# Routing attention and a squared-ReLU feed-forward: the attention stage's instruction order written out by hand for every engine

## The chip, the cores and the metric

The kernel runs on one core of a Trainium2 chip. The metric is device time in microseconds (us); times before are the median of three runs. Five engines work side by side, each through a queue of its own and in the order of that queue: TensorE (PE, with its weight loads as PEld), VectorE (DVE), ScalarE (ACT), GpSimd (POOL) and SyncE (SP), which here issues nearly all DMAs. An instruction that waits for another engine or a transfer holds up what stands behind it in its queue.

## The reference, cut to what matters

Queries and keys of each head are put into 16 clusters by their nearest centroid; a query attends to the keys of its own cluster. The result, with the heads side by side, goes through two matrices with a squared ReLU between.

```python
# q, k, v: (4, 8, 768, 64); centroids: (8, 16, 64); w_in: (512, 2048); w_out: (2048, 512)
q_assign = np.argmax(np.einsum('bhsd,hcd->bhsc', q_n, c_n), axis=-1)     # rows normalized
k_assign = np.argmax(np.einsum('bhsd,hcd->bhsc', k_n, c_n), axis=-1)
mask = q_assign[:, :, :, None] == k_assign[:, :, None, :]
scores = np.where(mask, scale * np.matmul(q, k.transpose(0, 1, 3, 2)), -1e9)
attn = softmax(scores)                       # over the keys
x = np.matmul(attn, v)                       # -> (3072, 512), heads side by side
r = np.maximum(x @ w_in, 0.0)
return (r * r) @ w_out
```

## The kernel before

Attention works on pairs of heads: `NG` = 16 pairs, numbered p, and three steps for each, so step t = 3p + ph with ph = 0, 1, 2. Steps 0 and 1 take 512 queries against half of the keys each, step 2 the other 256 queries against all. A step is: scores (`score_products`, tile sc, three PSUM tiles i = 0 to 2) and the mask added by a second product of one-hot codes (`mask_products`, from ohT), exponentials of the three tiles on ACT (tile ex), and one step later the products with v (`times_v`, tile av), whose result is copied to xT.

Around this, each pair needs:

- its transposed q and k (tile qkT). Pairs 0 and 1 are transposed on PE (`turn_first`, `turn`); the others are split into 16-bit words by ACT (`split_words`, tile flat), written out (words) and read back by a transposing DMA (`turn_words`).
- cluster numbers: `logits` (PE, tile lg, copied by ACT to lgs), then `number`: three transpositions on PE (lt), then on DVE a maximum (mx), two comparisons (best), a maximum (first) and a cast (ids_b). Pairs 0 and 1 turn the one-hot itself on PE (`turn_onehot`, oh to po to ohT). From pair 2 on `spread` transposes the numbers on PE (pb), ACT copies them (row), SP writes them out (far) and reads them back to all partitions (wide), and DVE compares them with each partition's own number (two operations, ohT).
- sums of the exponentials: step 0 on DVE (total), steps 1 and 2 begun on POOL (part) and merged by DVE. `add_up` adds them over the keys on PE (sm), takes the reciprocal on DVE (r), spreads it by DMA (far_r, rb) and scales xT.
- 16 blocks of `w_in` are loaded (w_raw) and rounded meanwhile, each with two ACT passes, three DVE passes and one POOL addition.

PSUM tiles pt, lg, lt, pb, sm and most po share one buffer (`misc`), so each waits until the one before is read.

Behind attention the feed-forward part runs batch by batch in the order 1, 2, 3, 0: `up` with seven half-size products in place of eight (`combine`), sums of blocks of x (x_t, DVE) and of `w_in` (w_s, POOL) as operands, and `down` in the same manner. During the first `up` the 16 blocks of `w_out` are rounded.

What sets the order: under `tc.manual_schedule(engines={PE})` PE's instructions run as written; the dictionary `between` lists what is put between scores and v products of each step (place 0) or behind the v products (place 1). The other engines' order is chosen by a scheduler from the program's order and priorities (`tc.high_priority(offset=200)` raises some), and `tc.issue_after` holds an instruction back behind another.

Of the kernel before, what the change touches and what calls it, by code (L numbers as in the profile page):

```python
# [12 lines left out]
U32 = mybir.dt.uint32  # L13
# [12 lines left out]
def kernel(  # L26
# [57 lines left out]
    BY_PE = 2  # L84
# [52 lines left out]
    def round_block(dst, w):  # L137
        dst = dst.bitcast(U32)
        lo, hi = w[:, :, 0], w[:, :, 1]
        nc.scalar.activation(out=dst.bitcast(F32), in_=hi.bitcast(F32), func=ACT.Abs)  # L140
        nc.scalar.activation(
            out=lo.bitcast(F32), in_=lo, func=ACT.Copy, bias=2.0, scale=2.0 ** -51
        )
        nc.vector.scalar_tensor_tensor(  # L144
            out=lo, in0=hi, scalar=0x80000000, in1=lo, op0=ALU.bitwise_and, op1=ALU.bitwise_or
        )
# [4 lines left out]
        nc.vector.tensor_scalar(  # L151
            out=dst, in0=hi, scalar1=3, scalar2=None, op0=ALU.logical_shift_left
        )
        dst, lo = dst.bitcast(I32), lo.bitcast(I32)
        nc.gpsimd.tensor_tensor(out=dst, in0=dst, in1=lo, op=ALU.add)

    def round_weights(i):
        round_block(weights[i][0] if i < N_IN else w_out[:, i - N_IN], raw_w.pop(i))
# [40 lines left out]
    constants = nc.vector.tensor_scalar(  # L199
        out=cl, in0=row_i[:, 1:2], scalar1=-1.0, scalar2=float(C), op0=ALU.mult, op1=ALU.add  # L200
    ).ins
# [9 lines left out]
    def centroids_norm():  # L211
        sq = once.tile([P, D], F32, name="cen_sq")
        ss = const.tile([P, 1], F32, name="cen_ss")
        with tc.issue_after(constants):
            nc.vector.tensor_tensor(out=sq, in0=cen, in1=cen, op=ALU.mult)
# [47 lines left out]
    def turn(pair, part, spare=False):  # L263
# [6 lines left out]
        nc.scalar.copy(out=qkT[pair][:, 4 * part : 4 * part + 4], in_=pt)  # L270
# [4 lines left out]
    last_exp = [None]  # L275

    def split_words(pair, which):
# [6 lines left out]
        for e in range(2):  # L284
            with tc.issue_after(last_exp[0]) if last_exp[0] else ExitStack():
                nc.scalar.copy(out=flat[:, :, :, D * e : D * (e + 1)], in_=src[:, e])  # L286
# [18 lines left out]
    def logits(pair):  # L305
        if pair >= NG:
            return
# [8 lines left out]
        with tc.high_priority(offset=200):  # L316
            nc.scalar.copy(out=lgs[pair], in_=lg)
# [3 lines left out]
    def number(pair):  # L321
        if pair >= NG:
            return
        lt = misc("lt", [P, NB, P])
        src = lgs.pop(pair)
        for i in range(NB):
            nc.tensor.transpose(out=lt[:, i], in_=src[:, i * P : (i + 1) * P], identity=ident)
# [4 lines left out]
        lt = lt.rearrange("p i (g c) -> p (i g) c", c=C)  # L332
# [4 lines left out]
        with tc.high_priority(offset=200):  # L337
            nc.vector.reduce_max(out=mx, in_=lt, axis=AX.X)
            nc.vector.tensor_tensor(out=best, in0=lt, in1=over_c(mx), op=ALU.is_ge)
            nc.vector.tensor_tensor(  # L340
                out=best, in0=best, in1=order.unsqueeze(1).to_broadcast([P, n, C]), op=ALU.mult
            )
            nc.vector.reduce_max(out=first, in_=best, axis=AX.X)
            if pair < BY_PE:
                nc.vector.tensor_tensor(
                    out=oh.rearrange("p i g e c -> p (i g e) c")[:, :, 0:C], in0=best,
                    in1=over_c(first), op=ALU.is_equal,
                )
            else:
                numbers[pair] = small.tile([P, 2, 4, NB], BF16, name="ids_b")  # L350
                nc.vector.tensor_copy(
                    out=numbers[pair].rearrange("p e g i -> p i g e"),
                    in_=first.rearrange("p (i g e) -> p i g e", i=NB, g=4),
                )

    def turn_onehot(pair, which, spare=False):
        if which == 0:
            ohT[pair] = ohtp.tile([P, 2, S], BF16, name="ohT")
        pt = misc("po", [P, NCH, P], BF16, spare=spare)
        for c in range(NCH):  # L360
            nc.tensor.transpose(
                out=pt[:, c],
                in_=oh[:, c % NB, 2 * which + c // NB].rearrange("p e c -> p (e c)"),
                identity=ident_b,
            )
        dst = ohT[pair][:, which]
        src = pt.rearrange("p c n -> p (c n)")
        if which == 0:
            nc.vector.tensor_copy(out=dst, in_=src)
        else:  # L370
            nc.scalar.activation(out=dst, in_=src, func=ACT.Copy, bias=-BIG, scale=BIG)

    def spread(pair):
        if pair >= NG:
            return
# [7 lines left out]
        wide = once.tile([P, 2, S], BF16, name="wide")  # L383
        ohT[pair] = ohtp.tile([P, 2, S], BF16, name="ohT")
        with tc.high_priority(offset=200):
            nc.scalar.copy(out=row, in_=pb)
            nc.sync.dma_start(far.rearrange("e r n -> (e r) n"), row)
            for e in range(2):
                nc.sync.dma_start(
                    wide[D * e : D * (e + 1)].rearrange("p g n -> p (g n)"),  # L390
                    far[e].rearrange("r n -> (r n)").partition_broadcast(D),
                )
        nc.vector.tensor_scalar(
            out=ohT[pair][:, 0], in0=wide[:, 0], scalar1=cl, scalar2=None, op0=ALU.is_equal
        )
        nc.vector.tensor_scalar(
            out=ohT[pair][:, 1], in0=wide[:, 1], scalar1=cl, scalar2=-BIG,
# [42 lines left out]
    def exponentials(t):  # L440
        ex[t] = []
        for i in range(3):
            ex[t].append(expp.tile([P, 2, 512], F32, name="ex"))
            last_exp[0] = nc.scalar.activation(  # L444
                out=ex[t][i], in_=sc[t][i], func=ACT.Exp, scale=SCALE
            ).ins
        sc.pop(t)
        pair, ph = divmod(t, 3)

        def add(eng, out, a, b):  # L450
            eng.tensor_tensor(out=out, in0=a, in1=b, op=ALU.add)  # L451

        e0, e1, e2 = ex[t]
        if ph == 0:
            total[pair] = endp.tile([P, 2, S], F32, name="total")
            dst = total[pair][:, :, 0:QA]
            add(nc.vector, dst, e0, e1)
            add(nc.vector, dst, dst, e2)
            return
        part = accp.tile([P, 2, 512], F32, name="part")  # L460
        add(nc.gpsimd, part, e0, e1)
        if ph == 1:
            dst = total[pair][:, :, 0:QA]
            add(nc.gpsimd, part, part, e2)
            add(nc.vector, dst, dst, part)
        else:
            add(nc.vector, part, part, e2)
            add(nc.vector, total[pair][:, :, QA:S], part[:, :, 0:QB], part[:, :, QB : 2 * QB])
# [4 lines left out]
    def scores(t):  # L473
        begin(t)
        for todo in pieces(t)[1]:
            score_products(t, todo)
            mask_products(t, todo)
        exponentials(t)
        if t % 3 == 2:
            for d in (qkT, ohT):  # L480
                d.pop(t // 3)
# [29 lines left out]

    def add_up(pair, sm):
# [14 lines left out]
        for e in range(2):  # L527
            nc.sync.dma_start(rb[D * e : D * (e + 1)], far[e].partition_broadcast(D))
        nc.sync.dma_start(seen[4 * pair : 4 * pair + 4], r)
        b, hp = divmod(pair, HP)  # L530
        x = x_of(b)[:, hp]
        nc.vector.scalar_tensor_tensor(
            out=x, in0=x, scalar=UP, in1=rb, op0=ALU.mult, op1=ALU.mult
# [5 lines left out]
    between = {}  # L539

    def put(t, place, work):
        between.setdefault((t, place), []).append(work)

    for i, place in ((0, 0), (1, 0), (2, 0)):
        put(0, 0, lambda i=i: turn(1, i, spare=i == 1))
    put(1, 0, lambda: logits(1))
    put(1, 1, lambda: number(1))
    put(2, 0, lambda: turn_onehot(1, 0))
    put(2, 1, lambda: turn_onehot(1, 1))
    put(3, 0, lambda: logits(2))  # L550
    put(3, 1, lambda: number(2))
    put(4, 0, lambda: spread(2))
    for p in range(NG - 1):
        t = 3 * p
        if p > 1:
            put(t, 1, lambda p=p: spread(p + 1))
        if p > 0:
            put(t + 1, int(p == 1), lambda p=p: add_up(p - 1, misc("sm", [P, TB])))
            put(t + 2, 0, lambda p=p: logits(p + 2))
            put(t + 2, 1, lambda p=p: number(p + 2))  # L560
    put(NT - 2, 0, lambda: add_up(NG - 2, misc("sm", [P, TB])))

    def transfers(t):
        pair, ph = divmod(t, 3)
        if ph == 0:
            load_qk(pair + 3)
            turn_words(pair + 2)
        else:
            split_words(pair + 3, ph - 1)
        if ph == 1:  # L570
            load_v(pair + 1)
        if ph == 2 and pair == HP:
            nc.sync.dma_start(x_far, xT.pop(0))
# [4 lines left out]
    logits(0)  # L578
    number(0)
    begin(0)  # L580
    score_products(0, pieces(0)[1][0])
    turn_onehot(0, 0, spare=True)
    turn_onehot(0, 1)
# [387 lines left out]
```

## Time and profile before

| | |
|---|---|
| median of 3 runs | 1008.78 us (1007.40 to 1010.06) |
| the profiled execution | 1009.22 us, of which the span of its instructions 1007.1 |
| PE busy | 942.0 us, 94% of the span |
| DVE, ACT, POOL busy | 554.8, 304.9, 271.7 us |
| mean granted TensorE clock | 0.977 |
| moved by DMA | 80.06 MB |

Start-up reaches to about 23 us (the scores of step 1), attention to 404.4, the first `up` to about 499, and the rest of the feed-forward part to the end. In rows of the profile L12 is line 12 of the kernel; "out<-in" names tiles; "xN" counts instructions. A view of stretches gives each engine's busy time, then the granted TensorE clock, the mean busy share of the 16 DMA engines and GB/s. In a time line a row has start, duration, engine, line and operation, and in brackets how long the engine stood idle before it and what ended that. In the list of waits a row has engine and line, whom it waited for, the total in us, how often, and the longest.

### The profile page before, as it was taken

The numbers are of one execution on the slowest core, as the hardware profiler recorded it, in microseconds if no ns is written. First come the engines' busy times: TensorE is split into PE (matmuls) and PEld (weight loads), VectorE is DVE, ScalarE is ACT, GpSimd is POOL, SyncE is SP. The second block draws the span as 40 slices with busy tenths as digits, with TensorE's granted clock in tenths as the row PEclk, the third lists the DMA queues.
The fourth block names the chain that finished last, engine by engine and source line by source line (L and its number), as shares of the span: only waits on it lengthen the run. The fifth ranks groups of instructions, "written<-read, shape, count | busy, mean of one in ns | idle before, by whom it ended". The sixth has DMA issues, their size and how long they took to land.

```text
span 1007.1 us, 11663 instructions
## 1 busy us (share of the span) xinstructions
PE 942.0 (94%) x4545; PEld 589.0 (58%) x4545; DVE 554.8 (55%) x809; ACT 304.9 (30%) x461; POOL 271.7 (27%) x217
## 2 busy tenths in 40 slices
PE   6889897988798999988899999999999999999997
PEld 4334343433343444544588755788655888556886
DVE  4356665656476575999822365622455532566321
ACT  4447564555556545443100011000111000111000
POOL 0224343434543344567000333001232002231000
PEclk9999998999999999999899999999999999999999
DMA  8537576757565720341100000000000000000000
GB/s 251 127 111 194 164 238 167 190 159 189 162 175 158 179 65 33 119 121 49 62 22 21 21 0 1 1 21 21 21 1 1 1 21 32 11 0 1 21 21 25
DMA packets 97912, 80.06 MB, mean 79 GB/s; under 512 B 53561, under 2 KB 86713, under 8 KB 97593
## 3 DMA queue, kind: packets, MB, share of 16 engines
q1 hardware_dynamic: 96136, 78.81, 26.9%
q8 instruction: 38, 0.62, 0.3%
q10 hardware_dynamic: 1712, 0.43, 0.2%
q14 instruction: 26, 0.20, 0.1%
HBM read 49.05 MB, written 19.06 MB: 68 GB/s over the span
## 4 chain that ended last, share of the span: by engine, by line
PE 66%; DVE 12%; issue 6%; DMA 6%; POOL 5%; ACT 4%; SPq 1%; ACTq 0%; DVEq 0%; POOLq 0%
PE bank L719 28%; PE bank L685 22%; PE sc L424 8%; PE av L502 5%; POOL part L451 3%; DMA rb<-far_r 2%; ACT ex L444 2%; DMA w_raw<-in_moe_w_out_dram 1%; PE sc L435 1%; DVE g L646 1%; DVE part L451 1%; ACT flat L286 1%; DVE w_raw L144 1%; DMA far<-row 1%; DMA far_r<-r 1%
## 5 line engine op out<-in xcount | busy, mean ns | idle before, releaser
L444 ACT ACTIVATE ex<-sc 128x1024 f32<-128x1024 f32 x144 | 139.2, 1027 | 117.7 <-PE sc L435 117.7
L646 DVE TENSOR_TENSOR g<-bank,g 128x384 f32<-128x384 f32 x192 | 103.4, 553 | 90.2 <-PE bank L685 89.1
L424 PE MATMUL sc<-qkT 64*128 64x512 f32 (+1 forms) x768 | 151.5, 529 | 1.0 <-ACT ex L444 1.0
L502 PE MATMUL av<-ex,v_raw 128*64 128x512 f32 (+1 forms) x768 | 137.1, 499 | 0.7 <-ACT xT L508 0.7
L719 PE MATMUL bank<-w_out,g 128*128 128x256 f32 x576 | 129.5, 384 | 4.4 <-DVE g L630 4.4
L674 POOL TENSOR_TENSOR w_s<-w_in 128x256 f32<-128x256 f32 x32 | 26.9, 842 | 364.6 <-PE bank L719 246.0
L719 PEld LDWEIGHTS bank<-w_out,g 128*128 128x128 f32 x576 | 111.0, 193 | 21.2 <-DVE g L630 4.8
L451 POOL TENSOR_TENSOR part<-ex 128x1024 f32<-128x1024 f32 x32 | 77.4, 2418 | 135.1 <-ACT ex L444 118.5
L646 DVE TENSOR_TENSOR osb<-bank,osb 128x256 f32<-128x256 f32 x72 | 29.4, 423 | 147.8 <-PE bank L719 137.2
L424 PEld LDWEIGHTS sc<-qkT 64*128 64x128 f32 x768 | 72.3, 196 | 57.5 <-issue 46.6
L502 PEld LDWEIGHTS av<-ex,v_raw 128*64 128x64 f32 x768 | 51.5, 138 | 76.5 <-issue 58.9
L685 PE MATMUL bank<-x_t,w_s 128*128 128x384 f32 x256 | 93.3, 487 | 3.1 <-DVE g L646 2.3
L685 PE MATMUL bank<-xT,w_in 128*128 128x384 f32 x256 | 93.5, 488 | 1.4 <-DVE g L646 1.4
L685 PE MATMUL bank<-xT,w_s 128*128 128x384 f32 x256 | 93.3, 487 | 1.1 <-POOL w_s L630 1.1
L719 PE MATMUL bank<-w_t,g 128*128 128x256 f32 x384 | 86.8, 379 | 0.0
L719 PE MATMUL bank<-w_t,g_s 128*128 128x256 f32 x384 | 86.8, 379 | 0.0
L719 PEld LDWEIGHTS bank<-w_t,g_s 128*128 128x128 f32 x384 | 73.0, 190 | 9.9
L719 PEld LDWEIGHTS bank<-w_t,g 128*128 128x128 f32 x384 | 73.0, 190 | 9.9
L650 ACT COPY osb<-bank 128x256 f32<-128x256 f32 x12 | 4.5, 372 | 219.6 <-PE bank L719 219.6
L685 PEld LDWEIGHTS bank<-x_t,w_s 128*128 128x128 f32 x256 | 48.4, 190 | 38.0 <-DVE g L646 3.5
L685 PEld LDWEIGHTS bank<-xT,w_s 128*128 128x128 f32 x256 | 48.4, 190 | 35.9 <-POOL w_s L630 1.7
L685 PEld LDWEIGHTS bank<-xT,w_in 128*128 128x128 f32 x256 | 48.2, 190 | 35.7 <-DVE g L646 2.7
(121 smaller groups left out, 1005.8 us busy)
## 6 DMA issues: line engine op xcount, KB each, us to landing
words<-flat SPq DMA_DIRECT2D x28, 384.0 KB
w_raw<-in_moe_w_in_dram SPq DMA_DIRECT2D x16, 512.0 KB
w_raw<-in_moe_w_out_dram SPq DMA_DIRECT2D x16, 512.0 KB
v_raw<-in_v_dram SPq DMA_DIRECT2D x16, 384.0 KB
rb<-far_r SPq DMA_DIRECT2D x32, 192.0 KB
out_dram<-osb SPq DMA_DIRECT2D x23, 256.0 KB
q_raw<-in_q_dram SPq DMA_DIRECT2D x14, 384.0 KB
k_raw<-in_k_dram SPq DMA_DIRECT2D x14, 384.0 KB
```

The costliest lines, as they stand in the source:

```text
L144: nc.vector.scalar_tensor_tensor(out=lo, in0=hi, scalar=0x80000000, in1=lo, op0=ALU.bitwise_and, op1=ALU.bitwise_or)
L286: nc.scalar.copy(out=flat[:, :, :, D * e : D * (e + 1)], in_=src[:, e])
L424: nc.tensor.matmul(sc[t][i][:, e, cols], lhsT=qkT[pair][rows, NCH + c], rhs=qkT[pair][rows, queries.start // P : queries.stop // P], start ...
L435: nc.tensor.matmul(sc[t][i][:, e, cols], lhsT=ohT[pair][rows, 1, c * P : (c + 1) * P], rhs=ohT[pair][rows, 0, queries], start=False, stop= ...
L444: last_exp[0] = nc.scalar.activation(out=ex[t][i], in_=sc[t][i], func=ACT.Exp, scale=SCALE).ins
L451: eng.tensor_tensor(out=out, in0=a, in1=b, op=ALU.add)
L502: nc.tensor.matmul(av[pair][D * e : D * (e + 1), 0:n], lhsT=raw_v[pair][:, e, c], rhs=e_t[i][:, e, cols], start=c == 0, stop=c == NCH - 1,)
L646: nc.vector.tensor_tensor(out=out, in0=bank, in1=to, op=ALU.add)
L650: nc.scalar.copy(out=c11, in_=bank)
L674: nc.gpsimd.tensor_tensor(out=s1, in0=a[1][0], in1=a[1][1], op=ALU.add)
L685: nc.tensor.matmul(bank, lhsT=operands[j][0][:, kk], rhs=operands[j][1][:, kk], start=(kk == 0), stop=(kk == H2 - 1),)
L719: nc.tensor.matmul(bank, lhsT=operands[j][0][:, f], rhs=operands[j][1][:, f], start=(f == 0), stop=(f == F2 - 1),)
```

## The change

The manual schedule now covers PE, DVE, ACT, POOL and SP, so in attention all five run in the order in which the loop over the steps issues. To make that order, functions are cut up:

- `number` is only the DVE part; its transpositions are `turn_logits`. `number(p + 1)` is issued at the beginning of step 0 of pair p, ahead of that step's scores, right behind `turn_logits` at the end of the step before; `spread(p + 1)` follows between the step's second and third exponential. The comparisons are a function `one_hot`, issued in step 2.
- The merges of POOL's sums are issued one step behind the sums (`merge_second` in step 2, `merge_third` in step 0 of the next pair, behind `number`). Scaling xT (`finish`) is issued in a later pair's step 0 than `add_up`.
- Rounding a block of `w_in` takes three steps, one engine in each (`round_1` ACT, `round_2` DVE, `round_3` POOL), one block for a pair, with the last three blocks in steps 40 to 47.
- `split_words` stands ahead of the exponentials of its step.
- Pair 2 too turns its one-hot on PE (`ONE_HOT` = 3), and `turn_onehot` does both halves between scores and masks. Of the first copies to qkT in `turn`, two of three go to DVE. v of pair 0 is loaded behind q and k of pair 2.
- The sums of x and the first two groups' sums of `w_in` for the first `up` are issued in the last two pairs.
- In the first `up` all four squared ReLUs of a group run on ACT; two of them were on DVE.

On DVE, where a pair's comparisons, sums and numbering meet (before, pairs around the stretch of 105 to 120 us):

```order
L522 RECIPROCAL r<-sm 128x384
L393 TENSOR_SCALAR ohT<-wide,cl 128x768
L396 TENSOR_SCALAR ohT<-wide,cl 128x768
L451 TENSOR_TENSOR total<-total,part 128x2x512
L144 SCALAR_TENSOR_TENSOR w_raw<-w_raw 128x512
L147 TENSOR_SCALAR w_raw<-w_in 128x512
L151 TENSOR_SCALAR w_in<-w_raw 128x512
L532 SCALAR_TENSOR_TENSOR xT<-xT,rb 128x768
L451 TENSOR_TENSOR part<-part,ex 128x1024
L338 TENSOR_REDUCE mx<-lt 128x24
L451 TENSOR_TENSOR total<-part 128x2x256
L339 TENSOR_TENSOR best<-lt,mx 128x384
```

The same place now:

```order
L543 RECIPROCAL r<-sm 128x384
L404 TENSOR_SCALAR ohT<-wide,cl 128x768
L407 TENSOR_SCALAR ohT<-wide,cl 128x768
L456 TENSOR_TENSOR total<-total,part 128x2x512
L347 TENSOR_REDUCE mx<-lt 128x24
L348 TENSOR_TENSOR best<-lt,mx 128x384
L349 TENSOR_TENSOR best<-best,order 128x384
L352 TENSOR_REDUCE first<-best 128x24
L360 CAST ids_b<-first 128x3x4x2
L456 TENSOR_TENSOR part<-part,ex 128x1024
L456 TENSOR_TENSOR total<-part 128x2x256
L556 SCALAR_TENSOR_TENSOR xT<-xT,rb 128x768
```

The rounding, the scaling of xT and the third step's merge stood ahead of the numbering or within it and now stand behind it; the comparisons and the second step's merge still stand ahead.

On PE, where the numbers are transposed (the scores of step 0 and their masks, sc<-ohT, stand ahead; lt stands ahead of those), before and now:

```order
L435 MATMUL sc<-ohT 128x512
L502 MATMUL av<-ex,v_raw 64x256 x12
L378 LDWEIGHTS ids_b
L378 MATMUL pb<-ident_b,ids_b 24x128
L424 MATMUL sc<-qkT 128x512 x6
```

```order
L446 MATMUL sc<-ohT 128x512
L387 LDWEIGHTS ids_b
L387 MATMUL pb<-ident_b,ids_b 24x128
L521 MATMUL av<-ex,v_raw 64x256 x12
L435 MATMUL sc<-qkT 128x512 x6
```

pb moved ahead of the v products of the step before.

On ACT at the start (steps 0 to 2), before and now:

```order
L444 ACTIVATE ex<-sc 128x1024 x3
L286 COPY flat<-q_raw 128x12x64 x2
L286 COPY flat<-k_raw 128x12x64 x2
L270 COPY qkT<-pt 128x512 x3
L444 ACTIVATE ex<-sc 128x1024 x2
L317 COPY lgs<-lg 128x384
```

```order
L453 ACTIVATE ex<-sc 128x1024 x3
L295 COPY flat<-q_raw 128x12x64 x4
L453 ACTIVATE ex<-sc 128x1024 x2
L279 COPY qkT<-pt 128x512
L453 ACTIVATE ex<-sc 128x1024
L323 COPY lgs<-lg 128x384
```

Four copies of words still stand between the first two steps' exponentials; of the copies to qkT one is left there.

The diff, cut to its core:

```diff
-    BY_PE = 2
+    BY_PE, ONE_HOT = 2, 3
...
     load_qk(0)
     load_qk(1)
+    load_qk(2)
     load_v(0)
-    load_qk(2)
...
-    manual.enter_context(tc.manual_schedule(engines={mybir.EngineType.PE}))
+    E = mybir.EngineType
+    manual.enter_context(
+        tc.manual_schedule(engines={E.PE, E.DVE, E.Activation, E.Pool, E.SP})
+    )
...
-        nc.scalar.copy(out=qkT[pair][:, 4 * part : 4 * part + 4], in_=pt)
+        (nc.scalar.copy if part == 2 else nc.vector.tensor_copy)(
+            out=qkT[pair][:, 4 * part : 4 * part + 4], in_=pt
+        )
...
+    def add_second(pair):
+        e0, e1, e2 = ex[3 * pair + 1]
+        part[pair] = accp.tile([P, 2, 512], F32, name="part")
+        add(nc.gpsimd, part[pair], e0, e1)
+        add(nc.gpsimd, part[pair], part[pair], e2)
+
+    def merge_second(pair):
+        dst = total[pair][:, :, 0:QA]
+        add(nc.vector, dst, dst, part.pop(pair))
...
+    def merge_third(pair):
+        p = part.pop(pair)
+        add(nc.vector, p, p, third.pop(pair))
+        add(nc.vector, total[pair][:, :, QA:S], p[:, :, 0:QB], p[:, :, QB : 2 * QB])
...
     rounded = loaded = 0
+    starts = [3 * p for p in range(1, 14)] + [40, 42, 45]
+    first_sums = []
+    x_early, w_early = x_sums(FEED[0]), []
     for t in range(NT + 1):
-        if t < NT:
-            if t:
-                scores(t)
-            transfers(t)
-            if t >= 6 and t % 2 == 0 and rounded < N_IN:
-                with tc.issue_after(last_exp[0]):
-                    round_weights(rounded)
+        p, ph = divmod(t, 3)
+        doing = t < NT
+        if ph == 0:
+            load_qk(p + 3)
+            if p + 2 > 2:
+                turn_words(p + 2)
+            if 2 < p + 1 < NG:
+                number(p + 1)
+            if p:
+                merge_third(p - 1)
+        elif ph == 1:
+            load_v(p + 1)
+        if t and loaded < rounded + 3:
+            load_weights(loaded)
+            loaded += 1
+        if p == 5 and ph == 1:
+            nc.sync.dma_start(x_far, xT.pop(0))
+        if doing:
+            scores(t)
...
+        if ph:
+            split_words(p + 3, ph - 1)
+        for i, begins in enumerate(starts):
+            if t == begins:
+                round_1(i)
+            elif t == begins + 1:
+                round_2(i)
+            elif t == begins + 2:
+                round_3(i)
                 rounded += 1
...
+        if ph == 2:
+            if p + 1 in wide:
+                one_hot(p + 1)
+            merge_second(p)
+        if doing:
+            exponential(t, 0)
+            exponential(t, 1)
...
+        if ph == 0 and 2 < p + 1 < NG:
+            spread(p + 1)
+        elif ph == 1 and p:
+            add_up(p - 1, misc("sm", [P, TB]))
+        elif ph == 2 and 2 < p + 2 < NG:
+            logits(p + 2)
+        if doing:
+            exponential(t, 2)
+        if ph == 0:
+            if p > 1:
+                finish(p - 2)
+            if doing:
+                add_first(p)
+        elif ph == 1:
+            add_second(p)
+        else:
+            add_third(p)
...
+        if t:
+            times_v(t - 1)
...
+        if ph == 2 and 2 < p + 2 < NG:
+            turn_logits(p + 2)
...
-                if n == 0 or (first and n == 1):
+                if n == 0 or b == FEED[0]:
                     nc.scalar.activation(out=to, in_=to, func=ACT.Relu)
                     nc.scalar.square(to, to)
```

More of the change, by code (lines that the diff above doesn't have):

```diff
@@ L284, in split_words @@
         for e in range(2):
[L285 to L286 removed]
+            nc.scalar.copy(out=flat[:, :, :, D * e : D * (e + 1)], in_=src[:, e])
         nc.sync.dma_start(
@@ L315, in logits, with turn_logits @@
         lgs[pair] = once.tile([P, TB], F32, name="lgs")
-        with tc.high_priority(offset=200):
-            nc.scalar.copy(out=lgs[pair], in_=lg)
+        nc.scalar.copy(out=lgs[pair], in_=lg)
+    lts = {}
+    def turn_logits(pair):
+        lts[pair] = misc("lt", [P, NB, P])
+        src = lgs.pop(pair)
+        for i in range(NB):
+            nc.tensor.transpose(
+                out=lts[pair][:, i], in_=src[:, i * P : (i + 1) * P], identity=ident
+            )
     numbers = {}
     def number(pair):
[L322 to L327, printed above, removed]
         n = NB * P // C
@@ L356, in turn_onehot @@
[L356 to L371, printed above, removed]
+                out=oh.rearrange("p i g e c -> p (i g e) c")[:, :, 0:C], in0=best,
@@ new lines, in number, with turn_onehot @@
+                in1=over_c(first), op=ALU.is_equal,
+            )
+        else:
+            numbers[pair] = small.tile([P, 2, 4, NB], BF16, name="ids_b")
+            nc.vector.tensor_copy(
+                out=numbers[pair].rearrange("p e g i -> p i g e"),
+                in_=first.rearrange("p (i g e) -> p i g e", i=NB, g=4),
+            )
+    def turn_onehot(pair):
+        ohT[pair] = ohtp.tile([P, 2, S], BF16, name="ohT")
+        for which in range(2):
+            pt = misc("po", [P, NCH, P], BF16, spare=which == 0)
+            for c in range(NCH):
+                nc.tensor.transpose(
+                    out=pt[:, c],
+                    in_=oh[:, c % NB, 2 * which + c // NB].rearrange("p e c -> p (e c)"),
+                    identity=ident_b,
+                )
+            dst = ohT[pair][:, which]
+            src = pt.rearrange("p c n -> p (c n)")
+            if which == 0:
+                nc.vector.tensor_copy(out=dst, in_=src)
+            else:
+                nc.scalar.activation(out=dst, in_=src, func=ACT.Copy, bias=-BIG, scale=BIG)
@@ L373, in spread @@
+    wide = {}
     def spread(pair):
-        if pair >= NG:
-            return
         n = 8 * NB
@@ L438, in mask_products, with exponential @@
                 )
[L440 to L468, printed above, removed]
+    def exponential(t, i):
+        ex.setdefault(t, []).append(expp.tile([P, 2, 512], F32, name="ex"))
+        nc.scalar.activation(out=ex[t][i], in_=sc[t][i], func=ACT.Exp, scale=SCALE)
@@ L474, in scores @@
         begin(t)
-        for todo in pieces(t)[1]:
+        pair, rounds, _ = pieces(t)
+        for todo in rounds:
             score_products(t, todo)
+            if t % 3 == 0 and pair < ONE_HOT:
+                turn_onehot(pair)
             mask_products(t, todo)
[L478 to L481, printed above, removed]
     av = {}
@@ L532, in add_up @@
         nc.vector.scalar_tensor_tensor(
-            out=x, in0=x, scalar=UP, in1=rb, op0=ALU.mult, op1=ALU.mult
+            out=x, in0=x, scalar=UP, in1=spread_out.pop(pair), op0=ALU.mult, op1=ALU.mult
         )
     x_far = dram_x.tile([P, KT, S], F32, name="x_far")
[L539 to L573, printed above, removed]
+    H2, F2, M2 = KT // 2, FT // 2, DM // 2
+    def sub(out, a, b, eng=nc.vector):
+        eng.tensor_tensor(out=out, in0=a, in1=b, op=ALU.subtract)
```

184 lines of the change are left out of this document (109 added, 75 removed).

## The prediction

> **What bounds the kernel now.** I read the page's busy times first, then stretches of the span by stage, then PE's waits, then the time line of one pair that stalls and one that does not.
>
> ```profile
> PE 942.0 (94%) x4545; PEld 589.0 (58%) x4545; DVE 554.8 (55%) x809; ACT 304.9 (30%) x461; POOL 271.7 (27%) x217
> core 0: us, PE busy (x) PEld busy (x) DVE busy (x) ACT busy (x) POOL busy (x), PEclk, DMA share, GB/s
> 0.00:23.00 23.00, 13.90 (x84) 8.96 (x84) 11.69 (x32) 11.96 (x17) 2.20 (x9) 0.99 0.82 247
> 23.00:404.40 381.40, 342.71 (x2214) 153.63 (x2213) 233.54 (x266) 214.72 (x290) 148.04 (x72) 0.95 0.56 154
> 404.40:503.70 99.30, 87.61 (x279) 51.66 (x278) 90.51 (x135) 37.55 (x71) 48.08 (x40) 0.97 0.27 89
> 503.70:1007.10 503.40, 497.76 (x1974) 374.73 (x1973) 219.02 (x376) 40.64 (x83) 73.37 (x96) 1.00 0.04 13
> 347.60:368.30 20.70, 20.70 (x142) 9.41 (x140) 15.72 (x15) 10.06 (x13) 7.10 (x3) 1.00 0.28 78
> 141.00:262.00 121.00, 104.08 (x671) 46.76 (x669) 75.72 (x95) 68.64 (x95) 47.91 (x23) 0.93 0.66 190
> ```
>
> TensorE bounds every stage, and the last half (503.7 to the end) has 5.6 us without it: nothing is to be had there. In attention from 23.0 to 404.4 PE is idle for 381.40 - 342.71 = 38.7 us, and the granted clock is 0.95. One pair of heads late in attention, 347.6 to 368.3, runs at clock 1.00 with PE never idle and takes 20.7 us: that is the floor of a pair. From one pb at 222.73 to another at 368.38 (both below) six pairs took 145.65 us, 24.3 each. In the first up-projection (404.4 to 503.7) PE is idle for 11.7 us and DVE is busy for 90.5 of 99.3.
>
> Who PE waits for, in attention and (fifth row) behind it, and what DVE waits for longest (engine and line, whom it waits for: us in all, times, longest):
>
> ```profile
> PE pb L378 <- DVE ids_b L351: 28.9, 9, 6.9
> PE po L361 <- DVE oh L345: 5.0, 2, 4.7
> PE pt L269 <- ACT qkT L270: 4.9, 1, 4.9
> PE lg L311 <- DVE r L522: 3.1, 1, 3.1
> PE bank L719 <- DVE g L630: 4.4, 1, 4.4
> DVE ohT L393 <- DMA wide<-far: 43.9, 13, 8.8
> ```
>
> Three quarters of attention's idle time is one wait: the transposition of the numbers (pb) for the last step of the numbering on DVE (ids_b). The time lines of DVE, POOL and PE in a pair that stalls say why DVE is late:
>
> ```profile
> 210.54 0.42 DVE L393 TENSOR_SCALAR ohT<-wide,cl 128x768 bf16<-128x768 bf16 x1 [5.54 <-DMA wide<-far]
> 214.03 2.04 POOL L155 TENSOR_TENSOR w_in<-w_in,w_raw 128x512 int32<-128x512 int32 x1 [5.93 <-DVE w_in L151]
> 216.04 2.37 POOL L451 TENSOR_TENSOR part<-ex 128x1024 f32<-128x1024 f32 x1
> 218.44 1.23 DVE L451 TENSOR_TENSOR part<-part,ex 128x1024 f32<-128x1024 f32 x1 [3.50 <-POOL part L451]
> 219.58 0.55 DVE L338 TENSOR_REDUCE mx<-lt 128x24 f32<-128x384 f32 x1
> 222.41 0.26 DVE L351 CAST ids_b<-first 128x24 bf16<-128x24 f32 x1
> 215.89 2.81 PE L502 MATMUL av<-ex,v_raw 128*64 128x256 f32 x24
> 222.73 0.23 PE L378 MATMUL pb<-ident_b,ids_b 128*24 128x128 bf16 x1 [4.03 <-DVE ids_b L351]
> ```
>
> DVE stands 5.5 us at the comparison with wide, which has not landed; the weight rounding behind it is late, POOL adds that block before the sums, DVE waits 3.5 us for POOL, and only then come mx to ids_b. PE has run out at 218.7. A long wait costs a second time; from the chain of work that ended last, the same twelve products, after a long wait and without one:
>
> ```profile
> 173.52 5.42 PE sc L424 x12
> 198.17 2.78 PE sc L424 x12
> ```
>
> **The change part by part.** The sum is made against the profiled execution, 1009.2 us (span 1007.1), 0.4 above the median of the runs shown.
>
> *Numbering first, comparison a step later.* lt now ends one step, the five operations follow at once on DVE, and pb comes after the next scores and masks. The unstalled pair gives the margin:
>
> ```profile
> 361.74 0.55 PE L327 MATMUL lt<-ident,lgs 128*128 128x128 f32 x3
> 362.22 2.85 PE L424 MATMUL sc<-qkT 64*128 64x512 f32 x12
> 365.64 2.81 PE L502 MATMUL av<-ex,v_raw 128*64 128x256 f32 x24
> 368.38 0.23 PE L378 MATMUL pb<-ident_b,ids_b 128*24 128x128 bf16 x1
> 357.97 1.21 DVE L451 TENSOR_TENSOR total<-total,part 128x1024 f32<-128x1024 f32 x1
> ```
>
> In the stalled pair mx to ids_b take 222.41 + 0.26 - 219.58 = 3.1 us with a 0.6 us sum in between, so 2.5 alone. PE has 365.64 - 362.22 = 3.4 us of scores and masks before the new place of pb (6.1 before, up to 368.38). The margin is 0.9 us if DVE is free when lt ends. Ahead of the numbering DVE now has the comparisons and the merge of the second step's sum: that merge ends at 359.2 in the unstalled pair, 3.1 us ahead of lt's end at 362.3. So I take the pb wait as gone, all 28.9; a slip of DVE under 3 us costs nothing.
>
> *Is there room on the other engines in 20.7 us?* The unstalled pair has DVE 15.7, ACT 10.1 and POOL 7.1, without splitting of q and k and without weights. Those add, by groups of 100 to 350 us:
>
> ```profile
> L286 ACT COPY flat<-k_raw 128x768 uint16<-128x768 uint16 x20 | 15.9, 858 | 0.0
> L141 ACT ACTIVATE w_raw<-w_raw 128x512 f32<-128x512 uint32 x17 | 11.6, 682 | 11.9 <-DMA w_raw<-in_moe_w_out_dram 11.9
> L144 DVE SCALAR_TENSOR_TENSOR w_raw<-w_raw 128x512 uint32<-128x512 uint32 x17 | 11.7, 687 | 3.6 <-ACT w_raw L141 3.6
> L155 POOL TENSOR_TENSOR w_in<-w_in,w_raw 128x512 int32<-128x512 int32 x15 | 25.7, 1713 | 101.2 <-DVE w_in L151 93.0 <-ACT flat L286 8.2
> ```
>
> ACT: four flats of 0.86 and two weight passes of 0.68, 4.8, to 14.9. DVE: one pass of 0.69 and two that I bound by it from above, at most 2.1, to 17.8. POOL: 1.7, to 8.8. All stay under 20.7, DVE with 2.9 to spare. The flats now stand ahead of a step's exponentials; these wait for the masks anyway (3.4 us behind the start of their step), and the flats' 1.7 run in that time. DMA: 0.66 of the 121 us of 141 to 262, at 24.3 a pair 5.0 pairs, is 16 us of a pair's 20.7; one weight block a pair instead of 17 in some ten takes it down. Full, but under the floor. On SP each pair now issues q, k, the transposing load and the weights, then far and wide, then v, words, far_r, rb, seen and words; wide may land 3.1 us later than in the unstalled pair before the numbering is touched. I cost SP at nothing with that cover; without it see the third rival. Scaling xT by rb a step or more late, and the sums of x and w_in near the end of attention, stand in nobody's way in attention, since PE reads them only in the up-projection. Cost nil, covered by DVE's 2.9 us a pair.
>
> [...] The row first: a comparison of 128x768 took 0.42 us at 210.54 beside an idle POOL, and 2.52 beside a running one:
>
> ```profile
> 355.54 2.52 DVE L396 TENSOR_SCALAR ohT<-wide,cl 128x768 bf16<-128x768 bf16 x1
> 355.46 2.37 POOL L451 TENSOR_TENSOR part<-part,ex 128x1024 f32<-128x1024 f32 x1
> ```
>
> [...] From rows alone: a second hold adds 2.52 - 0.42 = 2.1 to DVE's 17.8, which is 19.9, still under 20.7, and the merge that follows has to wait for the same sums. The sum stays as it is; the margin shrinks to 0.8. [...]
>
> *The clock.* 0.95 over 381.4 us is 19.1 us of lost clock; a part lies in idle time that is counted already. One stalled pair lost 5.42 - 2.78 = 2.6 in its scores; about eight such places, lighter ones at 1.5, agree with 15. I take 15, between 8 x 1.5 = 12 and 19.
>
> *The start.* Two of the three copies of pair 1's transposed q and k go to DVE, which is busy for 11.7 of the first 23 us, and scores of step 1 come ahead of the third:
>
> ```profile
> 18.67 2.91 ACT flat L286 x4
> 23.03 4.16 PE sc L424 x12
> ```
>
> PE waited 4.9 for a copy queued behind these four flats. Now step 1 waits for the exponentials of step 0 alone, which end where the flats begin, 18.7, and the first tile is free 2 us earlier: step 1 starts near 17.5 instead of 23.0. I take 4.5. The po wait of 4.7 goes in kind but comes back smaller: pairs 1 and 2 now transpose both halves of the one-hot in a row and wait for their copies, about 1.5 us each (0.8 us of copy and a sum ahead of it on DVE), lt of pair 2 holds its bank until DVE has read it (about 1.4 before lg), and step 2 waits about 1 for the late copy. With 0.6 of more PE work for pair 2: +6.
>
> *Behind attention.*
>
> ```profile
> 491.67 1.02 DVE L698 SCALAR_TENSOR_TENSOR g<-g 128x384 f32<-128x384 f32 x2
> 497.75 1.22 DVE L630 TENSOR_TENSOR g<-g,g_s 128x1024 f32<-128x1024 f32 x1
> ```
>
> 16 of L698 leave DVE for ACT, 8 us of DVE's 90.5 at 0.51 each, and ACT has 62 us to spare. DVE is some 3.7 us behind PE at 491; without that backlog the last sub (ends 498.97) comes 3 to 4 us earlier. Of the 4.4 wait I take 4, and 2 for the 0.97 clock: 6, between 0 (the end of g is then ACT's, two passes of 0.5 in a row more) and 9.
>
> The sum: idle 38.7 less 2 of small waits that stay, clock 15, start 4.5, behind attention 6: 62.2 off; 6 back in the first pairs, 2 for small new waits (0.15 us a pair): 54.2. 1009.2 - 54.2 = 955. Check by the floor: from 17.5 on, 47 steps of 20.7 / 3 and a last product of 2.8 end at 344.6, with the 8 back near 353 instead of 404.4: 51.8 off, where the sum has 48.2 for attention.
>
> **The rivals.** [...] *PE never waits from pair 1 on* and the first pairs' new waits fall into others' shadow: 8 less, 947. *It is slower:* SP is one queue, and in the hand-set order far and wide stand behind a transposing load that waits for the words to land. If wide lands 5 us late, the comparisons stop DVE, numbering and pb behind them, in every pair, and the clock falls each time as at 173.5. For it: DVE waited 8.8 us for wide once. Against it: DVE then had the weights and sums queued behind, now the numbering of this pair is done. 12 pairs x (3 + 1.7) = 56 eats all that was won; 5 us of wait and 2.6 of clock a pair, 91, gives 1046. It decides from 4.5 us a pair. *The order does nothing* in attention (PE waits as long for something else): 1009.2 less what comes behind attention, 1003 to 1009.
>
> **How the numbers follow.** The forecast 0.6, own range 946 to 964; the 2 us wait 0.2; no waits 0.13; slower 0.04; nothing 0.03. Range 942 to 985: leaves out the slow cases and the ends of the others. A difference under 0.3%, 3 us, can't be told from none. Faster 0.93, same 0.03, slower 0.04.
>
> **What would show it.** Right: the row pb <- ids_b nearly gone from PE's waits, idle of PE between the third pair and the end of attention under 6 us, a granted clock of 0.99 there, a pair in 20.7 to 21.0, attention over between 350 and 358. The start: scores of step 1 before 19. The transition: L719 <- DVE under 1 us. Wrong: PE waits of over 2 us that return each pair, on pb, lg or sm; DVE idle for wide over 3 us a pair; SP waiting for words ahead of far.

## The result and the profile after

The changed kernel takes 964.44 us (median, 962.59 to 966.05), the kernel before 1008.09 us (1007.39 to 1010.06) beside it: a ratio of 0.9563, 95% interval 0.9541 to 0.9586. That is 44 us off where the prediction had 54, and 9 us above its 955.

The stretches of the span, as they were shown of before (start and end, length, busy time of each engine with its instructions, granted clock, DMA share, GB/s); the profiled execution took 964.27 us:

```profile
core 0: us, PE busy (x) PEld busy (x) DVE busy (x) ACT busy (x) POOL busy (x), PEclk, DMA share, GB/s
0.00:19.30 19.30, 14.85 (x78) 9.70 (x78) 9.38 (x31) 6.54 (x10) 2.20 (x9) 0.91 0.80 233
19.30:66.50 47.20, 41.68 (x288) 19.20 (x287) 29.93 (x34) 32.14 (x43) 15.40 (x7) 1.00 0.76 185
66.50:335.00 268.50, 268.36 (x1817) 122.22 (x1817) 203.74 (x221) 178.71 (x242) 113.52 (x54) 1.00 0.71 186
335.00:360.20 25.20, 15.21 (x106) 6.98 (x102) 20.12 (x14) 10.24 (x13) 16.42 (x12) 0.84 0.12 38
87.00:107.70 20.70, 20.70 (x142) 9.41 (x140) 16.55 (x18) 14.10 (x20) 8.46 (x4) 1.00 0.83 199
365.50:465.50 100.00, 92.08 (x310) 56.11 (x309) 81.36 (x120) 51.64 (x103) 48.89 (x40) 1.00 0.27 89
```

From 66.5 to 335 us, thirteen pairs, PE is idle for 0.14 us at full clock, and a pair takes the 20.7 us of the floor. Then, in the 25 us before attention's last products, 10 us are idle and the clock is 0.84. Attention ends at 365.5 us instead of 404.4.

PE's waits:

```profile
PE av L521 <- ACT xT L527: 10.0, 1, 10.0
PE bank L748 <- DVE g L723: 3.6, 4, 1.2
PE sc L446 <- DVE ohT L378: 2.9, 2, 1.5
PE lg L318 <- issue: 2.5, 1, 2.5
PE bank L781 <- DVE g L566: 2.0, 1, 2.0
```

The row pb <- ids_b, 28.9 us of before, is gone. In its place as the longest stands a wait that the prediction has nowhere: one of 10.0 us, for a copy of xT on ACT. The time lines of DVE, the load queue (SPq), ACT and PE show how it comes about:

```profile
343.09 2.85 DVE L150 SCALAR_TENSOR_TENSOR w_raw<-w_raw 128x512 uint32<-128x512 uint32 x1
345.97 2.47 DVE L153 TENSOR_SCALAR w_raw<-w_in 128x512 f32<-128x512 f32 x1
349.23 2.54 DVE L543 RECIPROCAL r<-sm 128x384 f32<-128x384 f32 x1
351.80 0.52 SPq L546 DMA_DIRECT2D far_r<-r  x1
355.29 0.38 SPq L135 DMA_DIRECT2D w_raw<-in_moe_w_out_dram  x1
359.04 0.65 ACT L144 ACTIVATE w_raw<-w_raw 128x512 f32<-128x512 uint32 x1 [8.88 <-DMA w_raw<-in_moe_w_out_dram]
359.60 0.57 ACT L527 COPY xT<-av 128x512 f32<-128x512 f32 x1
360.21 5.39 PE L521 MATMUL av<-ex,v_raw 128*64 128x256 f32 x24 [10.01 <-ACT xT L527]
```

Read from below: PE needs a bank that ACT has not copied out; ACT stands for 8.88 us at the rounding of a w_out block that has not landed; its load was issued at 355.29, behind far_r, rb and seen in the load queue; far_r waited for r, and r stood on DVE behind the rounding of a w_in block that took 2.85 and 2.47 us where 0.69 and 0.43 are usual. Neither the load nor the rounding has anything to do with the copy. The rounding (L144) is written behind attention. It is no part of the hand-set order, so the scheduler was free to put it ahead of the copies:

```
197 L453 ACTIVATE ex<-sc 128x1024 x3
198 L144 ACTIVATE w_raw<-w_raw 128x512
199 L527 COPY xT<-av 128x512
...
204 L453 ACTIVATE ex<-sc 128x1024 x6
205 L144 ACTIVATE w_raw<-w_raw 128x512
206 L527 COPY xT<-av 128x512
207 L527 COPY xT<-av 128x256
```

(ACT's order in the changed kernel at two places near the end of attention; row 205 is the one that waited.) The wait has a second price: the 24 products behind it take 5.39 us instead of 2.81, at a granted clock of 0.50 from 360.2 to 365.6.

### The profile page after: what moved, and what is told of

Its sections match the earlier page's. It is cut to its first block, busy times and chain, and to the rows that moved or that the text cites. A ratio compares the mean times of both kernels' runs of the same rounds, so it can differ in the third digit from the quotient of the medians.

```text
span 962.4 us, 11697 instructions
## 1 busy us (share of the span) xinstructions
PE 928.6 (96%) x4556; PEld 585.8 (61%) x4556; DVE 564.5 (59%) x794; ACT 319.9 (33%) x491; POOL 269.9 (28%) x217
## 4 chain that ended last, share of the span: by engine, by line
PE 81%; DVE 8%; issue 4%; ACT 2%; DMA 2%; POOL 2%; ACTq 0%; SPq 0%; DVEq 0%; POOLq 0%
PE bank L781 29%; PE bank L748 23%; PE sc L435 11%; PE av L521 11%; PE sc L446 3%; DVE g L723 1%; PE lg L318 1%; PE sm L537 1%; DMA w_raw<-in_moe_w_out_dram 1%; DVE total L456 1%; DVE w_raw L150 1%; POOL w_out L165 1%; PE lt L331 1%; DVE w_raw L153 1%; DVE w_t L566 1%
## 5 line engine op out<-in xcount | busy, mean ns | idle before, releaser
L521 PE MATMUL av<-ex,v_raw 128*64 128x512 f32 (+1 forms) x768 | 137.0, 500 | 10.1 <-ACT xT L527 10.0
L435 PE MATMUL sc<-qkT 64*128 64x512 f32 (+1 forms) x768 | 140.9, 499 | 0.0
L781 PE MATMUL bank<-w_out,g 128*128 128x256 f32 x576 | 127.2, 379 | 2.0 <-DVE g L566 2.0
L781 PEld LDWEIGHTS bank<-w_out,g 128*128 128x128 f32 x576 | 109.4, 190 | 18.1 <-DVE g L566 2.4
L435 PEld LDWEIGHTS sc<-qkT 64*128 64x128 f32 x768 | 69.4, 188 | 56.4 <-issue 39.9
L521 PEld LDWEIGHTS av<-ex,v_raw 128*64 128x64 f32 x768 | 51.9, 139 | 80.4 <-issue 48.0
L781 PE MATMUL bank<-w_t,g_s 128*128 128x256 f32 x384 | 86.8, 379 | 0.0
L781 PE MATMUL bank<-w_t,g 128*128 128x256 f32 x384 | 86.8, 379 | 0.0
L781 PEld LDWEIGHTS bank<-w_t,g_s 128*128 128x128 f32 x384 | 73.0, 190 | 9.9
L781 PEld LDWEIGHTS bank<-w_t,g 128*128 128x128 f32 x384 | 73.0, 190 | 9.9
L727 ACT COPY g<-bank 128x384 f32<-128x384 f32 x32 | 15.2, 475 | 165.4 <-PE bank L748 165.4
```

What stands on the lines that cost most here:

```text
L435: nc.tensor.matmul(sc[t][i][:, e, cols], lhsT=qkT[pair][rows, NCH + c], rhs=qkT[pair][rows, queries.start // P : queries.stop // P], start ...
L521: nc.tensor.matmul(av[pair][D * e : D * (e + 1), 0:n], lhsT=raw_v[pair][:, e, c], rhs=e_t[i][:, e, cols], start=c == 0, stop=c == NCH - 1,)
L727: nc.scalar.copy(out=c11, in_=bank)
L781: nc.tensor.matmul(bank, lhsT=operands[j][0][:, f], rhs=operands[j][1][:, f], start=(f == 0), stop=(f == F2 - 1),)
```

## The experiments

Theory: the steady pairs are won by DVE's order, numbering first; what is missing is this one wait at a foreign instruction. Rivals: the gain is another engine's order; the wait at the end belongs to attention's own sums. The kernel before ran beside each of three groups of kernels, at 1008.07, 1011.38 and 1007.76 us; kernels of different groups are compared by their ratio to it.

**Numbering second.**

```diff
-            if 2 < p + 1 < NG:
-                number(p + 1)
             if p:
                 merge_third(p - 1)
+            if 2 < p + 1 < NG:
+                number(p + 1)
```

> In each pair the numbering of the next group is put behind the merge of the third bank instead of ahead of it, on DVE; the rest of the hand-set order stays. Theory (numbering first is what frees PE of its wait on ids_b): ids_b ends about 2.3 us later, at about 109.4 in the pair of 87 to 108 against a turn of TensorE that comes at 107.7, so that PE waits about 1.9 us in each of some 13 pairs: about 989 us. Rival (the slack of each pair takes it up): under 0.3 us of waiting in each pair and 964 to 968 us.

989.95 us (989.4 to 990.57), ratio 0.9819 (0.9794 to 0.9843), as expected. PE's wait, and DVE in the pair of 87 to 108 (here about 1 us later):

```profile
PE pb L387 <- DVE ids_b L360: 22.6, 12, 4.1
...
106.11 1.23 DVE L456 TENSOR_TENSOR part<-part,ex 128x1024 f32<-128x1024 f32 x1 [2.54 <-POOL part L456]
107.98 0.55 DVE L347 TENSOR_REDUCE mx<-lt 128x24 f32<-128x384 f32 x1
110.33 0.26 DVE L360 CAST ids_b<-first 128x24 bf16<-128x24 f32 x1
```

DVE waits for POOL's sum with the numbering behind it, and the wait on pb is back twelve times, 1.9 us each. These two lines are worth 0.0256 of 1008, 26 us. The other half of the new order, pb ahead of the v products on PE, was not tried by itself.

**All engines but DVE by hand; then only TensorE and DVE; then these and ACT.**

```diff
-        tc.manual_schedule(engines={E.PE, E.DVE, E.Activation, E.Pool, E.SP})
+        tc.manual_schedule(engines={E.PE, E.Activation, E.Pool, E.SP})   # the first
+        tc.manual_schedule(engines={E.PE, E.DVE})                        # the second
+        tc.manual_schedule(engines={E.PE, E.DVE, E.Activation})          # the third
```

> All engines but DVE follow the hand-set order; DVE's operations go as the scheduler puts them. Theory (DVE's order is what frees TensorE): most of the 2 us of waiting per pair comes back, 985 to 1010 us. Rival (the others' order does it): 953 to 970 us.

> Only TensorE and DVE follow the hand-set order; ACT, GpSimd and the load queue go as the scheduler puts them. Theory (the gain of the steady pairs is DVE's order): the pb wait stays away and the time is 953 to 970 us. Rival (the order of ACT's copies or of the load queue is needed as well): waits of 0.5 us or more come back in each pair and the time is 975 to 1000 us.

> TensorE, DVE and ACT follow the hand-set order; GpSimd and the load queue go as the scheduler puts them. Theory (after the run with two engines, whose waits were for ACT's copies of ohT and lgs, 20.6 and 16.7 us): those waits go with ACT's order, and the time is 955 to 968 us. Rival (the load queue's or GpSimd's order is needed too): waits of over 1 us on wide, flat or the second pass of sums come back in several pairs, 975 us or more.

Without DVE's order: 1021.67 us, ratio 1.0102 (1.0077 to 1.0128), slower than before and above the range expected. PE's wait:

```profile
PE pb L387 <- DVE ids_b L360: 40.7, 12, 5.6
```

With TensorE and DVE alone: 1001.78 us, ratio 0.9906 (0.9882 to 0.9929). Neither range holds this time. The rival had the cause, ACT's order, but not its form: the waits are not in each pair. PE's waits, and one stretch of the pairs:

```profile
PE sc L446 <- ACT ohT L380: 20.6, 3, 8.7
PE lt L331 <- ACT lgs L323: 16.7, 4, 6.0
...
147.00:335.00 188.00, 188.00 (x1272) 85.22 (x1270) 139.63 (x151) 101.56 (x136) 81.14 (x44) 1.00 0.53 131
```

From 147 to 335 us PE never stops, so the orders of TensorE and DVE are enough for a steady pair; but the copies of ohT and lgs, queued on ACT behind flats and exponentials, cost 37 us, all but one wait of 5.4 before 147 us. With ACT by hand too they go, but for one of 5.3 us for lgs behind 147 us: 959.23 us, ratio 0.9518 (0.9503 to 0.9532), within the range expected. That is better than the changed kernel, which was run again beside it:

> The changed kernel again, on the chip of this call, to stand beside the two others: 962 to 966 us, with one wait of about 10 us at the end of attention.

965.96 us, ratio 0.9581 (0.9568 to 0.9595), with the wait at 11.0 us. So the gain doesn't need the hand-set orders of GpSimd and of the load queue; without them the time is some 6 us less, with 0.7 us of waiting for the xT copy at the end of attention.

**Fewer squares on ACT.**

```diff
-                if n == 0 or b == FEED[0]:
+                if n == 0 or (b == FEED[0] and n == 1):
```

> In the first block of the feed-forward only the first two of the relus go to ACT, as in the kernel before; the others are on DVE again. Theory (that part of the change is worth what the wait for the last square was): the wait of PE on DVE's g grows by 3 to 6 us and the time is 967 to 970 us. Rival (DVE has room there): 963.5 to 965.5 us.

971.03 us (970.5 to 972.68), ratio 0.9636 (0.9615 to 0.9658), 1 us above the range expected: 0.0073 or 7 us more than the changed kernel. PE's waits in the up-projection and at its end:

```profile
PE bank L748 <- DVE g L723: 5.5, 6, 1.6
PE bank L781 <- DVE g L566: 4.4, 1, 4.4
```

Against 3.6 and 2.0 that is 4.3 us, of which 1.0 goes off for two smaller waits on banks there (2.3 us in the changed kernel, 1.3 here). The profiled executions differ by 6.8, and 2.2 of pb waits and 0.6 more at the end of attention are in this one without having to do with the part. So it is worth 7 us at most, and by the waits alone 3.3.

**Earlier sums of w, so that they don't hold the rounding; and an earlier third load.**

```diff
-        if NT - 3 <= t < NT - 1:
+        if NT - 5 <= t < NT - 3:      # the first
```
```diff
-    starts = [3 * p for p in range(1, 14)] + [40, 42, 45]
+    starts = [3 * p for p in range(1, 14)] + [40, 41, 43]      # the second
```

> GpSimd's early sums of w are put at steps 43 and 44 instead of 45 and 46, so that they don't hold DVE's rounding of the last w_in block in step 46. Theory (the held rounding delays r, and r the third w_out load): the three rounding operations fall from 2.85, 2.47 and 0.83 us to under 1 us each, r ends about 4 us earlier, PE's wait on the xT copy falls from 10 to 5 or 6 us, and the time is 957 to 960 us. Rival (the load is late for another reason): the wait stays near 10 us and the time within 1 us of 964.

> The last two starts of the w_out loads move from steps 42 and 45 to 41 and 43, so that the third of these loads is issued ahead of step 46's far_r and rb on the load queue; nothing else changes. Theory (ACT's rounding of the third w_out block stands ahead of the last two xT copies and waits for this late load): the 10.0 us wait of PE on the xT copy falls under 1 us, the granted clock stays full there, and the time is 951 to 953 us. Rival (ACT's xT copies wait for something of their own, such as the rounding of w_in on DVE): the wait stays at 8 us or more and the time 962 to 966 us.

Both missed: 963.97 us, ratio 0.9567 (0.9540 to 0.9595), and 962.39, ratio 0.9545 (0.9524 to 0.9565). Both did what they were to do, and neither gained by it. With the earlier sums, DVE, ACT, and PE's wait:

```profile
348.29 0.69 DVE L150 SCALAR_TENSOR_TENSOR w_raw<-w_raw 128x512 uint32<-128x512 uint32 x1
349.01 0.43 DVE L153 TENSOR_SCALAR w_raw<-w_in 128x512 f32<-128x512 f32 x1
340.80 0.66 ACT L144 ACTIVATE w_raw<-w_raw 128x512 f32<-128x512 uint32 x1 [7.46 <-DMA w_raw<-in_moe_w_out_dram]
...
PE av L521 <- ACT xT L527: 8.0, 2, 5.2
```

The rounding is back to 0.69 and 0.43, so POOL's sums had held it. The last wait is 2.84 instead of 10; a new one of 5.17 stands at 337, at the second w_out block. With the earlier third load, ACT and PE:

```profile
341.65 0.67 ACT L144 ACTIVATE w_raw<-w_raw 128x512 f32<-128x512 uint32 x1 [5.57 <-DMA w_raw<-in_moe_w_out_dram]
343.28 5.49 PE L435 MATMUL sc<-qkT 64*128 64x512 f32 x12 [4.34 <-ACT ex L453]
```

The last wait is 0.69; this one of 4.34, and twelve scores of 5.49 us, where those at 17.27 took 2.85, are new. Here the scheduler put the third L144 ahead of a step's exponentials, where its load, issued at 338.1, had not landed. With the earlier sums ACT's order is that of the changed kernel; there it is the second load that comes late. The loads of w share three buffers, and POOL's addition that ends the use of one now stands behind the sums: the load was issued at 337.19, while in the changed kernel the addition ended at 329.49 and the load was issued at 329.52. In all three kernels an L144 in front of a copy or of exponentials hands the lateness of its load on to PE. What has to be changed is its place, not the load's.

**The rounding placed by hand.** L144 becomes a function of its own, called for the three blocks behind attention's last products and inside the hand-set order (in this and the next kernels lines lie 5 to 9 further down: L143 is the old L144, L526 the old L521):

```diff
+    for i in range(N_IN, N_IN + 3):
+        round_lo(i)
     manual.close()
```

> The first rounding operation of the three w_out blocks on ACT (one of 0.66 to 0.70 us each, which waits for the block's load) is placed by hand behind attention's last xT copy, where the scheduler had put two of them among attention's copies and exponentials and one ahead of the last two xT copies; the loads' places stay. Theory (after the run with the earlier third load, in which the wait was 0.7 us at the end but 4.3 us appeared at another of these operations): none of the three can hold an xT copy or an exponential, PE waits under 1.5 us in all from 330 us to the end of attention, the granted clock stays full there, and the time is 951 to 954 us. Rival (the waits of the end of attention come from late r or late sums, and only show at ACT): 5 us or more of waiting stay, 958 to 964 us.

961.9 us (958.3 to 965.39), ratio 0.9520 (0.9491 to 0.9549), where 951 to 954 was expected. PE's wait at the end, the end of attention, and the 100 us behind it:

```profile
PE av L526 <- ACT xT L532: 0.7, 1, 0.7
...
335.00:355.10 20.10, 19.41 (x142) 9.31 (x138) 17.42 (x11) 9.53 (x11) 16.68 (x13) 1.00 0.01 2
355.10:455.00 99.90, 89.58 (x284) 52.87 (x283) 85.45 (x124) 53.45 (x106) 49.13 (x41) 0.97 0.30 98
```

The mechanism came as the theory had it: 0.7 us of waiting, full clock, attention over at 355.1 instead of 365.5. The time did not: the span is 958.0, only 4.4 less. In the next 100 us PE is busy for 2.5 us less than in the changed kernel's row above, at a clock of 0.97 instead of 1.00; some 6 of the 10.4 us are given back there. An estimated 3 to 4 of these 6 are clock (0.03 of these 99.9 us; 0.04 of the 96.4 from 365.6 to 462.0). Part of that can be chance: from 365.6 to 462.0 the changed kernel has 1.00 and the kernel with the earlier third load, whose program behind attention is the same, 0.98, an estimated 1.9 us.

**The same with the early third load and cnT copied ahead of the last part of pair 0's turned k, twice; and the rounding between the last two xT copies.**

```diff
+            if which == 1:
+                centroids_turned()
...
+        if t == NT - 1:               # the last kernel only, in place of the loop behind the products
+            for i in range(N_IN, N_IN + 3):
+                round_lo(i)
```

> The placed rounding as in the run beside it, the third w_out load ahead of step 46's far_r, and the copy of cnT between the two copies of the first pair's turned q and k on DVE. Theory: the wait on cnT (1.34 us) goes to under 0.5, so that the start is about 1 us shorter, and the first rounding of the third block no longer holds the first copy of g; 949 to 952 us. Rival (the cnT copy only moves the wait to the copy behind it): the same as the run beside it within 0.5 us.

> The run with the placed rounding and the early third load again, on the chip of this call: 955 to 959 us, some 7 us under the changed kernel.

> As the run with the placed rounding and the early third load, but the three operations stand between attention's last two xT copies (where ACT was idle for 2.9 us) instead of behind both. Theory (some 6 us of the end's gain was given back in the first block of the feed-forward, where waits grew by 2.4 us and the clock fell to half in two stretches of 3.4 us, because ACT's three operations there stood ahead of its first copy of g): ACT's order behind attention is again that of the changed kernel, the waits there are 7 to 8 us, and the time is 951 to 954 us. Rival (the give-back has another cause): within 1.5 us of the earlier run's 957 us.

957.23 us, ratio 0.9480 (0.9455 to 0.9505), above the 949 to 952 expected, and again 956.13, ratio 0.9486 (0.9473 to 0.9499): the best of all kernels, 9.8 us under the changed kernel beside it. In place of the wait of 1.34 us for cnT stands one of 0.48 for ACT's copy of qkT; how much of the gain over the kernel with the rounding alone is this and how much the load was not separated. Between the copies: 960.07, ratio 0.9508 (0.9486 to 0.9529), above both ranges, with executions from 954.41 to 961.19. ACT's order behind attention was the old one again, and the give-back stayed: from the end of attention to the end of the span it is 603.2 us, against 596.9 in the changed kernel and 602.9 with the rounding behind the copies. So ACT's three operations are not needed for it. What the traces show in its place (not tested by a run of its own): the kernel with three engines ends attention at 361.1, this one at 356.1, but DVE's first additions of g come at the same time. DVE there, in the run with three engines:

```profile
359.27 1.23 DVE L456 TENSOR_TENSOR part<-part,ex 128x1024 f32<-128x1024 f32 x1 [2.51 <-POOL part L456]
365.57 1.67 DVE L723 TENSOR_TENSOR g<-bank,g 128x384 f32<-128x384 f32 x3
```

and POOL and DVE with the rounding between the copies:

```profile
351.40 0.73 POOL L593 TENSOR_TENSOR w_s<-w_in 128x256 f32<-128x256 f32 x1
355.15 2.37 POOL L463 TENSOR_TENSOR part<-ex 128x1024 f32<-128x1024 f32 x1
357.55 1.23 DVE L463 TENSOR_TENSOR part<-part,ex 128x1024 f32<-128x1024 f32 x1 [4.34 <-POOL part L463]
360.29 1.89 DVE L155 SCALAR_TENSOR_TENSOR w_raw<-w_raw 128x512 uint32<-128x512 uint32 x3
365.39 2.79 DVE L732 TENSOR_TENSOR g<-bank,g 128x384 f32<-128x384 f32 x5
```

POOL does sums of w from 351.4 on, ahead of the last pair's last sum; DVE waits 4.34 us for that sum, then has 1.9 us of rounding more. PE is 5 us earlier, DVE is not, and it is DVE that frees the banks; ACT's first copy of g, too, waits 1.40 us for a sum on DVE. By this reading the 10 us wait of the changed kernel was the cover of these sums. With the rounding behind both copies DVE is late by less (its first addition of g comes 6.6 us behind the end of attention, against 4.4 in the changed kernel and 9.3 here), so the cause of the give-back stays open in part.

## Why the prediction was right, and where it was off

*pb and numbering first (all 28.9 off).* Right. DVE and PE in the pair of 87 to 108 and, fourth row, in the next:

```profile
104.40 0.56 DVE L347 TENSOR_REDUCE mx<-lt 128x24 f32<-128x384 f32 x1 [1.76 <-PE lt L331]
106.76 0.26 DVE L360 CAST ids_b<-first 128x24 bf16<-128x24 f32 x1
107.72 0.23 PE L387 MATMUL pb<-ident_b,ids_b 128*24 128x128 bf16 x1
120.74 2.32 DVE L456 TENSOR_TENSOR total<-total,part 128x1024 f32<-128x1024 f32 x1
```

ids_b is ready 0.7 us ahead of pb (said: 0.8 to 0.9), and DVE waits 1.76 us for lt. Beside operations of POOL (from 118.25 to 120.60 and from 120.56 to 121.98) L407 took 2.51 us from 118.31 on, where its median is 0.41, and the merge 2.32 instead of 1.21; in the next pair the merge ends at 123.06 and mx starts at 125.09, so 2.0 of the 3.1 us are left. A wait of 2 us in each pair (chance 0.2), a slow load queue and an order without effect fall in this trace. In other executions, though, pb waited in one to four pairs; 3.1 us in all in the second run of the changed kernel, where wide came late, on DVE for instance

```profile
291.19 0.42 DVE L404 TENSOR_SCALAR ohT<-wide,cl 128x768 bf16<-128x768 bf16 x1 [7.58 <-DMA wide<-far]
```

This is the slow load queue's mechanism, too rare to decide. So the nil of the pb wait is that of the first trace; the 2 us that the sum has for small waits are nearer to the others.

*Room on the engines.* DVE 16.55, ACT 14.10 and POOL 8.46 of 20.7 us against 17.8, 14.9 and 8.8; DMA 0.83 of 20.7, 17.2 us where 16 was said.

*First pairs, +6.* From 19.3 to 66.5 us PE is idle for 47.20 - 41.68 = 5.5 us, with the two ohT waits (2.9) and the lg bank (2.5) as named; that one was put at 1.4. The profile names no releaser for lg, but DVE's last reading of lt ended at 56.47 and lg began at 56.57.

*Small waits, +2.* 0.14 us.

*The clock, 15.* From the scores of step 1 to the end of attention PE was busy for 342.71 us, and now for 41.68 + 268.36 + 15.21 + 5.39 = 330.6: 12.1 less. With the 2.6 lost behind the new wait and the 0.6 of more work that the sum allows for pair 2, the old losses of clock come to an estimated 15.3. The size was right.

*The start.* Step 1 starts at 19.33, not 17.5 or "before 19". The order was right; in this execution step 0's scores took 4.16 us, with the granted clock at half from 11.0 to 14.4. In the kernel with the earlier third load, whose start is the same, they took 2.85, at 1.00 from 9.5 to 16.0, and the row of step 1 comes at

```profile
17.27 2.85 PE L435 MATMUL sc<-qkT 64*128 64x512 f32 x12
```

*Behind attention.* L781 <- DVE is 2.0 us, where the prediction had it under 1; so 2.4 of 4. From the end of attention to the end of the span it is 596.9 us instead of 602.7, 5.8 less where the sum has 6. The squares' own experiment puts them between 3.3 and 7.

*The step that failed.* Attention gave 404.4 - 365.5 = 38.9 us of the 48.2 in the sum. What failed is "Scaling xT by rb a step or more late, and the sums of x and w_in near the end of attention, stand in nobody's way in attention ... Cost nil, covered by DVE's 2.9 us a pair". The cover is that of a steady pair. In the last two there are more sums on POOL, DVE's rounding is held by them, r and the third w_out load come late, and an operation outside the hand-set order carries this to PE. Measured: 10.0 us of wait and 5.39 - 2.81 = 2.6 of clock, 12.6 in all. Without these, attention would have ended at 365.5 - 12.6 = 352.9, where the check by the floor said 353, and the time, 964.4 - 12.6 = 951.8, would lie 3 us under the forecast. As the placed rounding shows, not all of that could be had by taking the wait away.

## What to carry to other kernels

A hand-set order is only as good as its borders: look in each engine's built order for operations of the next phase that a scheduler has mixed in, and ask of each whether it can wait for a load while the critical engine waits behind it. Move such an operation, not the load it waits for; in the run that moved the load, the wait came back in another place (4.34 us). Price the last turns of a loop by themselves, and before you take a wait away, look at what it covers on the other engines.

## What the runs showed of the hardware

Looked at in steps of 0.1 us, the granted clock of the changed kernel stands at half twice: for 3.4 us from 11.0 to 14.4, and at the end of attention for 13.6, four times 3.4, from 352.3 to 366.0, beginning 2.1 us after PE's last product. In the kernel before, in steps of 0.2 us, there are nine such stretches: six of 3.4 us, two of 6.8 and one of 10.2. Whether one comes with a wait of 2 to 2.5 us differs between executions. Around the same waits, 2.5 us for lg near 55 us and 2.0 at the first product of the down-projection, the changed kernel and then the one with the earlier third load:

```profile
52.00:62.00 10.00, 7.49 (x57) 3.53 (x55) 7.85 (x9) 3.93 (x5) 4.67 (x3) 1.00 0.90 209
455.00:462.00 7.00, 5.53 (x26) 4.89 (x27) 1.41 (x2) 0.00 (x0) 0.00 (x0) 1.00 0.00 0
```

```profile
52.00:62.00 10.00, 7.50 (x32) 2.54 (x33) 7.28 (x9) 3.75 (x5) 2.61 (x2) 0.83 1.13 230
453.00:460.00 7.00, 5.43 (x17) 4.51 (x18) 1.52 (x2) 0.00 (x0) 0.00 (x0) 0.76 0.00 0
```

The 0.17 of 10.00 us and the 0.24 of 7.00 by which the second kernel's clock is short of full come to 1.7 us each, an estimated 3.4 us at half clock. So the wait of 2.0 us came with such a stretch in one execution and without one in the other.

The program needn't differ: in the ten executions of the changed kernel the mean granted clock was 0.989 to 0.992; 0.003 of 964 us is an estimated 2.9. One stretch of 3.4 us at half clock costs 1.7 where PE has work, so a difference of 2 or 3 us between two executions of one kernel can be this alone.
